# Other landing times, load order and ranks for a list-scheduled attention and feed-forward kernel

## The chip, the cores and the metric

The kernel runs on one core of a Trainium2 chip. It uses five engines: TensorE (PE) for matmuls, VectorE (DVE), ScalarE (ACT) and GpSimd (POOL) for everything elementwise, and SyncE (SP) whose queue issues nearly all DMA transfers. Each engine works through its own list of instructions strictly in order and waits for the others by semaphores. The metric is the device time of one execution in microseconds (us); the median of three runs stands below.

## The reference

The inputs are `q`, `k`, `v` of shape (8, 8, 576, 64), `w_in` (512 x 2048) and `w_out` (2048 x 512), all float32. The output is 4608 x 512 float32.

```python
scores = scale * np.matmul(q, k.transpose(0, 1, 3, 2))
rel = pos[:, None] - pos[None, :]
mask_plain = (rel >= 0) & (rel < 32)                      # heads 0 to 3
mask_dil = (rel >= 0) & (rel < 128) & (rel % 4 == 0)      # heads 4 to 7
attn = softmax(where(masks, scores, -1e9))
x = matmul(attn, v)  # (8, 8, 576, 64) -> (4608, 512)
h = x @ w_in
g = np.maximum(0.01 * h, h)
return g @ w_out
```

## The kernel before

The work is done batch by batch: 8 batches of 8 heads and 576 tokens. A pair of batches gives 1152 columns of the transposed attention output `xt`, which is cut into three chunks of 384 tokens, so there are 12 chunks. For each chunk the up-projection (`up`, matmuls of 128 x 384 at L1073) multiplies `xt` by 16 blocks of `w_in` and ACT bends the result into `gt` (L1084); the down-projection multiplies `gt` by `w_out` and the result is evicted into `osb` or `vst` and stored. The first four tiles of 128 tokens go down in the plain way (`down`, L1244: 16 matmuls of 512 columns in four parts, then an eviction by DVE at L1252). The others go in groups of four through a seven-product scheme (`group`, L1335) that uses sums of blocks of `w_out` (`weight_sums`, L1274). The last four chunks also go up by seven products (`up_seven`, L1157).

Batches 0 and 1 are handled apart ("early"): their q and k are turned by TensorE (L729) and copied into `slots` (L646 on ACT, L648 on DVE), the scores of a unit are made in one bank (L869, L888, L872), exponentiated by ACT (L894), multiplied with v (L929, L949, L939; L917 makes the sums), and normalised through a logarithm and an exponential on ACT (L961, L963) and a product on DVE (L967) that writes `xt`. The 64 tokens beyond 512 of each head come apart: `load_rest` loads those of q and k of all heads in one transfer each, and the last tokens of v of the dilated heads.

All loads arrive as float32 in staging tiles (`stg` for q and k, `vst` for v, parts of `gt`, `wst` and `xt[1]` for the weights) and are cast to float16 by POOL, DVE or ACT (L344, L342). `w_in` comes in eight pieces of 512 KB (`load_w(0..7)`), `w_out` in eight more (`load_w(8..15)`); some pieces share a home buffer with an earlier one and wait until its casts are done. A mask table `late_m` is loaded by SP (`t_near`, L365) and spread by six copies on POOL or ACT (L375).

No order is written out by hand. Every operation is a task with the engines that may do it, an estimated duration, a latency, its dependencies and a priority. `_Plan.run` schedules these tasks as a list scheduler would: for each engine it takes the ready task of lowest priority value, models one DMA server with a service time per transfer (`took`), and gives the landing time of a transfer as its end on the server plus 1.1 us and a lateness. `load` has a factor `slow` on the service time; `load_w` passes `W_SLOW` for the first four pieces of `w_in`. Then `latest` goes backwards through the schedule, ranks every compute task by how late it may start, adds a random disturbance if the seed is not 0, and the plan is run again, once for each entry of `SEEDS`. DMA tasks keep the priorities they were given.

The priorities of the first loads are given by the string `FIRST`, one letter for each step: `b` a group of four heads of batch 0 (q and k), `v` its v, `c` and `y` the same for batch 1, `i` a piece of w_in, `o` a piece of w_out, `0` and `1` the rest tokens of batch 0 and 1. The first `b` and `c` are the dilated heads. `RANKS`, `WHEN`, `MOE`, `W_SUMS` and `SUMS` are first priorities of attention units, of the later batches, of the chunks and of the weight sums; `NEAR` is the priority of the load of `late_m`. Last, where the plan leaves TensorE idle before `WARM` = 62 us of planned time, filler matmuls on a tile of zeros (`warm`, L1558) are put into its list; a few more stand at the beginning (L1454). The resulting lists are what the engines execute.

Of the kernel before, what the change touches and what calls it, by code (L numbers as in the profile page):

```python
# [16 lines left out]
LATE = 7.0  # L17
HOLD = 5.0
W_ENG = ("POOL", "DVE", "ACT")
WHEN = (4.52, -1.03, 5.19, 90.96, 96.86, 93.61, 150.56, 174.24)  # L20
WARM = 62.0
W_SLOW = 1.25
SEEDS = (0, 0, 0, 0, 0, 0, 0, 0, 0, 775539)
AFTER = -1495.0
NEAR = -1498.63
FIRST = 'bvbviiii0iiiicycyoooooooo1'
RANKS = ((12.88, -25.12), (25.21, -10.26), (-1.14, 23.42), (33.7, 4.07))


def _constants():  # L30
# [180 lines left out]
def kernel(  # L211
# [48 lines left out]
    def dram(t, off, *dims):  # L260
        return bass.AP(tensor=t.tensor, offset=t.offset + off, ap=[list(d) for d in dims])
# [67 lines left out]
    def load(queue, dst, src, n, size, deps, prio, slow=1.0):  # L329
        eng = ENG[queue]  # L330
        over = getattr(src if prio == -3000 else dst, "ap", [[0, 0]])[0][1]
        return plan.dma(queue, 0.7 if n == 1152 else 0.62 if over == 64 else 0.45, took(n, size) * slow, deps,
                        lambda e: eng.dma_start(dst, src), prio,  # L333
                        LATE if prio > -1500 + len(FIRST) else 0.8 if prio >= AFTER else 0.0)

# [28 lines left out]
    t_bias = load("ACT", con[:, 128:M_KEEP], const_d[:, 128:M_KEEP], 128, 2 * NBIAS, [], -1498.5)  # L364
    t_near = load("SP", late_m[:, NLATE - 160:NLATE], late_d, 128, 320, [], NEAR)  # L365
    t_con = add("ACT", 0.21, 0.22, [t_bias],
# [161 lines left out]
    def load_rest(b, prio):  # L528


        _, r_old = ring("REST", 1, r_users := [])
        sn, s_old = ring("STG", NST, s_users := [])
        st, lo = stg[sn], []
        for o, src in ((0, q), (1, k)):
            lo.append(load("SP", at(st, 0, 128, o * 256, [1, 256]),
                           dram(src, b * H * HS + 512 * D, [HS, 8], [4 * D, 16], [1, 256]),
                           128, 1024, s_old, prio))
        c = cast(at(rest, 0, 128, 0, [128, 8], [D, 2], [1, D]),
                 at(st, 0, 128, 0, [D, 8], [0, 2], [1, D]), 1024, lo + r_old, prio, W_ENG)
        s_users.append(c)  # L540
        vs, v_old, v_users = v_late[b]
        spread = bass.AP(tensor=vs.tensor, offset=vs.offset + 1024,
                         ap=[[4 * vs.ap[0][0], 16], [256, 4], [1, 256]])
        lv = load("SP", spread,
                  dram(v, (b * H + 4) * HS + 512 * D, [4 * D, 16], [HS, 4], [1, 256]),
                  64, 1024, v_old + [t_vr], prio)
        for vi in (2, 3, 0, 1):
            vt, d_users = kept[b, vi]
            c_v = []
            if vi >= 2:  # L550
                c_v = [cast(at(vt, 0, 64, 0, [1024, 2], [128, 4], [1, D]),
                            at(vs, 0, 64, 1024 + (vi - 2) * 256, [512, 2], [D, 4], [1, D]), 512,
                            [lv] + d_users, prio + 30, W_ENG)]
                v_users += c_v
            visits[b, vi, 1] = rest, [c], r_users, vt, c_v + seen_ones[b, vi], d_users
# [3 lines left out]
    def load_w(n, prio):  # L559
# [6 lines left out]
        if n >= 8:  # L566
            x = 1024 * (n - 8)
            t = load("SP", st, dram(moe_w_out, 128 * x, [2 * DM, 128], [1, 1024]), 128, 4096, old, prio)
            for i in range(2):
# [6 lines left out]
        t = load("SP", st, dram(moe_w_in, n % 4 * 128 * DFF + x, [DFF, 128], [1, 1024]), 128, 4096, old, prio,  # L576
                 W_SLOW if n < 4 else 1.0)
        g, h = n % 4 // 2, n % 2
# [15 lines left out]

    segs = {b: [(0, 96, 384 * (b % 2)), (96, 48, 768 + 192 * (b % 2))] for b in range(EARLY)}
    chunks = [(m, 384 * i, 384) for m in range(B // 2) for i in (0, 1, 2)]
    MOE = 36.21
    PLAIN = 4
    tiles = [(c, tt) for c in range(len(chunks)) for tt in range(3)]
    groups = [tiles[i:i + 4] for i in range(PLAIN, len(tiles), 4)]  # L600
# [1 line left out]
    for m, x, n in chunks:  # L602
        begins.append(begins[-1] + MOE * n / 384)

# [485 lines left out]
        return t_p  # L1090

    SEVEN = (8, 9, 10, 11)
    W_SUMS = 440.23
    u_sums, u_last = {}, {}

    def w_quarter(k, f):
# [2 lines left out]
    def up_sums(old, raw):  # L1099
# [3 lines left out]
        def make(n, dst, x, y, op, deps):  # L1103
            u_sums[n] = shared("DVE", 1.16, 0.2, deps,
                            lambda e: ENG[e].tensor_tensor(out=dst, in0=x, in1=y, op=op),
                            W_SUMS, 0.0, "T")
        w_all = [c for j in range(NJ) for b in w_in_t[j] for c in b]
# [162 lines left out]
    def weight_sums():  # L1270
        w_all = sum((w_out_t[j] for j in range(NJ)), [])

        def minus(n, dst, x, y, deps):
            t_sum[n] = shared("DVE", 1.16, 0.2, deps, lambda e: nc.vector.tensor_tensor(  # L1274
                out=dst, in0=x, in1=y, op=ALU.subtract), SUMS, 0.0, "T")
        minus(1, flat(sums[1]), w_block(0, 1), w_block(0, 0), w_all + w_used[9] + w_used[10])
# [4 lines left out]

    roles = [0, 1]
    last_of = {}
    SUMS = -41.62

    def group(four, acts, at_time, split):

# [175 lines left out]
    ranks = {}  # L1463
    for n, step in enumerate(FIRST):
        seen = FIRST[:n].count(step)
        if step in "io":
# [31 lines left out]
    for m in range(B // 2):  # L1498
        for b in (2 * m, 2 * m + 1):
            if b < EARLY:  # L1500
                attend(b, 0, *RANKS[2 * b])
                if b == 0:
# [3 lines left out]
                    clear_slots(range(4, NT), -700, x_done[0, 0][-1:])  # L1506
                attend(b, 1, *RANKS[2 * b + 1])
            else:
                a, z = WHEN[b - 1], WHEN[b]
                attend(b, None, a, (z - a) / 4)  # L1510
# [40 lines left out]
    order = plan.run()  # L1551
    for seed in SEEDS:
        plan.latest(seed)
# [67 lines left out]
```

## Time and profile before

| | us |
|---|---|
| median of 3 runs | 306.95 (306.02 to 307.24) |
| the profiled execution | 307.09 |
| its span | 305.2 |
| TensorE busy | 293.0 |
| VectorE busy | 249.9 |
| ScalarE busy | 225.1 |
| GpSimd busy | 118.8 |

The span is the time from the first to the last instruction of the profiled execution. Busy times of TensorE include the fillers, and matmuls overlap in their pipeline, so that their ends are modelled; a busy TensorE is no proof of useful work. 47.22 MB are moved by DMA in the execution, 23.39 MB of them in the first 90 us. In the groups of instructions, the up-projections at L1073 hold 97.6 us of TensorE, the seven-product down-projections at L1335 47.2 us with w_out and 16.4 us with the sums in `wst`, and the four plain tiles at L1244 16.1 us. The longest waits in all are POOL's for turned tiles (34.8 us) and ACT's for up-projections (21.3 us); TensorE itself waits little, at most 1.5 us in any one group.

### The profile page before, as it was taken

The page shows a single profiled execution, that of the slowest core. Times are in us where ns is not written, and L with a number is a line of the kernel's source. Part 1 is how long each engine was busy: PE and PEld are TensorE (multiplying, and loading weights), DVE is VectorE, ACT ScalarE, POOL GpSimd, SP SyncE. Part 2 cuts the span into 40 slices and gives each one's busy share as a digit, 9 for nine tenths or more (in the row PEclk, how much of TensorE's full clock was granted, in tenths as well). Part 3 has the DMA queues.
Part 4 walks back from the last instruction along what each step waited for, and adds up shares of the span by engine and source line. Part 5 has one row for each costly group of instructions (what it writes and reads, how often), then busy time and mean ns, then how long its engine had stood idle before and what let it go on. Part 6 is the DMA issues. An engine that isn't in the chain of part 4 may idle for free.

```text
span 305.2 us, 8114 instructions
## 1 busy us (share of the span) xinstructions
PE 293.0 (96%) x3039; PEld 230.5 (76%) x3039; DVE 249.9 (82%) x477; ACT 225.1 (74%) x549; POOL 118.8 (39%) x164
## 2 busy tenths in 40 slices
PE   8788889999999999999999999999999999999994
PEld 4444544566898778778777787778999999999983
DVE  6778785749899989998998899999998868586842
ACT  4989985789898885787677778667568888777420
POOL 6148643058936826936845753771000000000000
PEclk9999999999999999999999999999999999999998
DMA  7999999899799697757994898782212110121034
GB/s 248 336 320 393 312 378 200 171 180 202 173 174 195 134 173 157 138 130 141 177 159 138 148 189 153 143 175 78 73 55 80 42 37 0 37 71 35 11 111 123
DMA packets 157159, 47.22 MB, mean 155 GB/s; under 512 B 137408, under 2 KB 154560, under 8 KB 157120
## 3 DMA queue, kind: packets, MB, share of 16 engines
q1 hardware_dynamic: 156544, 46.39, 64.6%
q8 instruction: 24, 0.39, 0.6%
q10 hardware_dynamic: 576, 0.32, 0.4%
q14 instruction: 15, 0.12, 0.1%
HBM read 37.24 MB, written 9.44 MB: 153 GB/s over the span
## 4 chain that ended last, share of the span: by engine, by line
PE 78%; DVE 6%; ACT 5%; DMA 4%; SPq 3%; issue 1%; DVEq 0%
PE hps L1073 22%; PE fps L1335 21%; PE tp L1335 8%; PE hps L1157 7%; PE fps L1244 5%; PE ops L1016 4%; PE ops L1157 3%; DMA wst<-in_moe_w_in_dram 3%; SPq L333 3%; PE sps L1157 2%; ACT gt L1084 1%; PE sps L1010 1%; PE sps L1016 1%; DVE ee L1026 1%; PE ops L1010 1%
## 5 line engine op out<-in xcount | busy, mean ns | idle before, releaser
L1073 PE MATMUL hps<-xt,w_in 128*128 128x384 f16 (+1 forms) x556 | 97.6, 307 | 1.7 <-DVE w_in L344 1.2
L1335 PEld LDWEIGHTS <-gt 128*128 128x128 f16 x768 | 72.3, 98 | 9.0
L1084 ACT ACTIVATE gt<-hps 128x384 f16<-128x384 f32 (+1 forms) x139 | 62.2, 455 | 22.6 <-PE hps L1073 21.3
L1073 PEld LDWEIGHTS <-w_in 128*128 128x128 f16 x576 | 50.1, 98 | 25.4 <-ACT w_in L342 1.8
L1335 PE MATMUL fps<-w_out,gt 128*128 128x256 f16 x368 | 47.2, 272 | 0.0
L687 POOL COPY slots<-turned 64x512 f16<-64x512 f16 (+1 forms) x36 | 25.7, 715 | 41.2 <-DVE turned L697 34.8
L344 POOL CAST v_all<-vst 64x1152 f16<-64x1152 f32 (+3 forms) x29 | 34.8, 1201 | 7.6 <-DMA vst<-in_v_dram 6.9
L344 POOL CAST nat<-stg 128x576 f16<-128x576 f32 (+1 forms) x44 | 33.8, 789 | 8.0 <-DMA stg<-in_k_dram 3.6
L1026 DVE TENSOR_TENSOR ee<-ee,late_m 128x384 f16<-128x384 f16 (+1 forms) x48 | 29.0, 619 | 3.8 <-ACT ee L1023 3.5
L1045 DVE TENSOR_TENSOR xt<-ops,rc 128x288 f16<-128x288 f32 x48 | 26.5, 553 | 3.7 <-PE ops L1016 2.3
L1157 PEld LDWEIGHTS <-w_in 128*128 128x128 f16 x256 | 21.8, 98 | 0.4
L1364 ACT COPY stg<-fps 128x512 f32<-128x512 f32 (+1 forms) x24 | 12.7, 530 | 11.9 <-PE fps L1335 11.8
L1037 ACT ACTIVATE rc<-rc 128x288 f32<-128x288 f32 x48 | 20.9, 447 | 0.6
L717 DVE STREAM_TRANSPOSE slots<-nat 64x576 f16<-64x576 f16 x24 | 18.4, 767 | 0.4
L697 DVE STREAM_TRANSPOSE turned<-nat 128x576 f16<-128x576 f16 (+1 forms) x24 | 17.5, 735 | 0.4 <-ACT nat L342 0.2
L1157 PEld LDWEIGHTS <-stg 128*128 128x128 f16 x192 | 16.6, 98 | 0.3
L1321 DVE TENSOR_TENSOR gt<-gt 128x1024 f16<-128x1024 f16 x21 | 16.2, 773 | 0.6 <-PE fps L1335 0.6
L1016 PEld LDWEIGHTS <-v_all 128*128 128x128 f16 x240 | 14.5, 98 | 3.0 <-issue 0.2
L1016 PE MATMUL ops<-ee,v_all 128*128 128x96 f16 (+2 forms) x240 | 16.4, 199 | 0.1
L1335 PE MATMUL fps<-wst,gt 128*128 128x256 f16 x128 | 16.4, 273 | 0.0
L967 DVE TENSOR_TENSOR xt<-ops,rc 64x192 f16<-64x192 f32 (+1 forms) x30 | 10.6, 352 | 6.9 <-ACT rc L963 6.4
L1244 PE MATMUL fps<-w_out,gt 128*128 128x512 f16 x64 | 16.1, 380 | 0.0
(151 smaller groups left out, 594.2 us busy)
## 6 DMA issues: line engine op xcount, KB each, us to landing
stg<-in_q_dram SPq DMA_DIRECT2D x48, 144.0 KB, 3.4
stg<-in_k_dram SPq DMA_DIRECT2D x48, 144.0 KB, 3.1
vst<-in_v_dram SPq DMA_DIRECT2D x12, 288.0 KB, 4.1
vst<-in_v_dram SPq DMA_DIRECT2D x24, 128.0 KB, 2.7
gt<-in_moe_w_in_dram SPq DMA_DIRECT2D x5, 512.0 KB, 8.2
xt<-in_moe_w_out_dram SPq DMA_DIRECT2D x3, 512.0 KB, 5.7
gt<-in_moe_w_out_dram SPq DMA_DIRECT2D x3, 512.0 KB, 8.0
vst<-in_v_dram SPq DMA_DIRECT2D x3, 384.0 KB, 6.0
```

The source lines that it names most:

```text
L344: ENG[e].tensor_copy(out=dst, in_=src)
L687: lambda e: (nc.scalar.copy if e == "ACT" else nc.gpsimd.tensor_copy)(out=at(to, p0, p1, p0 if to is qb else 0, *dims), in_=at(fr, p0, p1, ...
L717: lambda e, p0=64 * h: nc.vector.transpose(at(qb, p0, p0 + 64, p0, [128, 9], [1, 64]), na[p0:p0 + 64, S:2 * S]), prio))
L1016: nc.tensor.matmul(at(bk, 0, 128, o, *dims), stationary(s), et[:, c:c + n], start=i == 0, stop=i == len(parts) - 1, skip_group_check=True)
L1026: lambda e: nc.vector.tensor_tensor(out=et[:, 0:w], in0=et[:, 0:w], in1=mk, op=ALU.mult), prio + 0.1)
L1037: lambda e: nc.scalar.activation(out=rt[:, 0:NQ], in_=rt[:, 0:NQ], func=AF.Exp, scale=-1.0),
L1045: lambda e: nc.vector.tensor_tensor(out=dst, in0=at(ot, 0, 128, 0, *src), in1=at(rt, 0, 128, 0, *src), op=ALU.mult), prio + 0.2)
L1073: nc.tensor.matmul(ht[:, 0:n], at(w_in, 0, 128, i * DFF + j // 2 * 256 + j % 2, [2, 128]), at(xt[m % 2], 0, 128, i * 1152 + x0 + x, [1, n] ...
L1084: lambda e: nc.scalar.activation(out=gt[c % NG][:, j * n_c + x:j * n_c + x + n], in_=ht[:, 0:n], func=AF.Prelu, alpha=0.01),
L1157: nc.tensor.matmul(bk[:, 192 * jj:192 * jj + 192], w(i, 2 * jp + jj), x(i), start=first and jj == 0 and i == 0, stop=jj == 1 and i == 1, s ...
L1244: nc.tensor.matmul(ft, g[:, j * n_c + tt * 128:j * n_c + tt * 128 + 128], w_out[:, j * DM:j * DM + DM], start=(j == 0), stop=(j == NJ - 1))
L1335: nc.tensor.matmul(bk[:, x:x + HN], tl[:, off + j * step:off + j * step + 128], rhs(j), start=first and x == 0 and j == 0, stop=j == HJ - ...
```

## The change

The list is told longer times for two kinds of loads: the factor on the first four pieces of `w_in` goes from 1.25 to 1.5, and the loads of the rest tokens of q and k get a factor of 1.8 (1.0 before). The constants that set the first priorities, and the seeds, have other values. In `FIRST`, the loads of batch 1 were `c y c y`, then eight `o`, then the rest tokens; now they alternate with w_out's: `c o o c o y o o o o o y 1`. The priority of the load of `late_m` now puts it ahead of all others on SP's queue. No operation is added or removed, except that the list holds 35 fillers at L1558 instead of 31; what each task computes is the same.

```diff
-WHEN = (4.52, -1.03, 5.19, 90.96, 96.86, 93.61, 150.56, 174.24)
+WHEN = (10.27, -7.79, -8.5, 83.93, 95.4, 101.07, 152.79, 178.8)
 WARM = 62.0
-W_SLOW = 1.25
-SEEDS = (0, 0, 0, 0, 0, 0, 0, 0, 0, 775539)
+W_SLOW = 1.5
+SEEDS = (0, 0, 0, 0, 0, 0, 695242, 808820, 89207, 493360)
 AFTER = -1495.0
-NEAR = -1498.63
-FIRST = 'bvbviiii0iiiicycyoooooooo1'
-RANKS = ((12.88, -25.12), (25.21, -10.26), (-1.14, 23.42), (33.7, 4.07))
+NEAR = -1507.43
+FIRST = "bvbviiii0iiiicoocoyoooooy1"
+RANKS = ((15.99, -23.22), (36.98, -8.41), (1.15, 24.48), (33.14, 4.11))
...
-                           128, 1024, s_old, prio))
+                           128, 1024, s_old, prio, 1.8))
...
-    MOE = 36.21
+    MOE = 39.96
...
-    W_SUMS = 440.23
+    W_SUMS = 379.53
...
-    SUMS = -41.62
+    SUMS = -51.79
```

Since every task goes through the list, the change moves instructions on all engines. On SP: the load of `late_m` is the first of all instead of the fourth; the first two w_out pieces stand after the first q and k of batch 1, the third after the second q and k, then the dilated heads' v, five more w_out pieces, the plain heads' v, and the rest tokens. On TensorE: the first w_out product stands after 18.99 us of matmul work (at 2.4 columns per ns) instead of 24.00, and the parts of the first two tiles alternate; all of chunk 0's plain tiles stand before chunk 1's first up-projection. On ACT: five copies of `late_m` instead of two, before the first cast of k; five casts of q and k of early batches instead of one; two casts of each kind of v instead of one. On DVE: seven casts of q and k instead of ten, two of the rest tokens instead of one, and the first two weight sums around the first tile's eviction.

## The prediction

> **What bounds the kernel now.** I read the busy row by slices first, then a table by stages, then the order of TensorE's work in the start, then the GpSimd casts that show when weights land.
>
> ```profile
> span 305.2 us, 8114 instructions
> ...
> PE   8788889999999999999999999999999999999994
> ...
> DMA  7999999899799697757994898782212110121034
> ```
>
> The span is 305.2 us; this execution took 307.09 us, so 1.9 us lie around it, and it stands 0.14 us above the median of 306.95. TensorE is full from the seventh of the 40 slices (46 us) nearly to the end; the DMA engines are full from the second to the seventh (7.6 to 53 us). The stages (length, then busy time of PE, PE's weight loads, DVE, ACT, POOL, then clock, DMA share, GB/s):
>
> ```profile
> 10.00:20.00 10.00, 7.77 (x84) 4.29 (x80) 6.91 (x20) 9.31 (x30) 2.10 (x3) 1.00 1.08 311
> 20.00:30.00 10.00, 8.63 (x64) 4.61 (x65) 8.55 (x21) 8.22 (x19) 8.19 (x12) 1.00 1.05 379
> 30.00:40.00 10.00, 8.68 (x81) 5.13 (x78) 7.92 (x21) 9.80 (x24) 5.77 (x11) 1.00 1.03 317
> 40.00:50.00 10.00, 9.44 (x86) 5.05 (x85) 7.31 (x20) 7.36 (x24) 3.48 (x6) 1.00 1.03 339
> 50.00:60.00 10.00, 9.96 (x71) 5.28 (x70) 6.40 (x13) 6.03 (x15) 1.22 (x2) 1.00 0.85 158
> 60.00:70.00 10.00, 10.00 (x83) 6.05 (x82) 5.43 (x15) 8.70 (x21) 4.74 (x10) 1.00 0.93 172
> 90.00:120.00 30.00, 29.34 (x339) 23.58 (x338) 28.51 (x47) 24.80 (x62) 16.90 (x20) 1.00 0.89 168
> ```
>
> From 60 us on TensorE only works, with 0.66 us lost in 90 to 120, where VectorE is busy 28.51 of 30. What can move the time is how much work TensorE has behind it when its queue becomes solid. I count that work from the matmuls in instruction order, at 2.4 columns per ns (a row of 8 x 384 columns takes 1.30 us, 2.36 per ns); the whole program has 268.05 us, without the filler products on `warm`, whose time is lost time. The order of TensorE around the first w_out products:
>
> ```profile
> 42.28 0.61 PE L729 MATMUL tp<-con,nat 128*128 128x128 f16 x8 [0.29 <-DVE slots L648]
> ...
> 45.28 0.39 PE L1558 MATMUL fps<-warm 128*128 128x512 f16 x1
> ...
> 46.49 1.04 PE L1244 MATMUL fps<-w_out,gt 128*128 128x512 f16 x4
> ...
> 53.52 0.59 PE L1558 MATMUL fps<-warm 128*128 128x512 f16 x2
> 53.95 1.03 PE L1244 MATMUL fps<-w_out,gt 128*128 128x512 f16 x4
> 54.82 1.46 PE L1073 MATMUL hps<-xt,w_in 128*128 128x384 f16 x8
> ```
>
> Work done: 6.83 us when the first up-projection starts (19.29), 16.64 at 35.4, 24.00 at 46.49, 31.57 at 54.82, 36.6 at 60.0. So 12.5 us are lost before 19.29, 6.3 more up to 35.4, and 4.5 between 35.4 and 54.82 (19.4 of time, 14.9 of work). In that last stretch TensorE has only batch 1's attention, in small steps behind ACT and DVE copies, and the rest of chunk 0's up-projections; w_out comes late:
>
> ```profile
> 38.47 0.61 POOL L344 CAST w_out<-xt 128x512 f16<-128x512 f32 x1 [0.46 <-DMA xt<-in_moe_w_out_dram]
> 39.70 0.61 POOL L344 CAST w_out<-wst 128x512 f16<-128x512 f32 x1 [0.61 <-DMA wst<-in_moe_w_out_dram]
> ...
> 47.53 0.61 POOL L344 CAST w_out<-xt 128x512 f16<-128x512 f32 x1 [0.98 <-DMA xt<-in_moe_w_out_dram]
> 50.13 0.61 POOL L344 CAST w_out<-xt 128x512 f16<-128x512 f32 x1 [1.99 <-DMA xt<-in_moe_w_out_dram]
> 51.55 0.61 POOL L344 CAST v_all<-vst 64x512 f16<-64x512 f32 x1 [0.80 <-DMA vst<-in_v_dram]
> ```
>
> Each cast waits for its own landing: one 512 KB piece per 1.2 to 1.3 us, the last of eight at 50.1, batch 1's last v tokens at 51.5.
>
> **The start of batch 0 (cost).** The mask load late_m goes from fourth to first on SP's queue. SP's issues are 0.51 us apart (0.75, 1.26, 1.77), so the first two q loads and the first k load come 0.5 us later; those behind keep their places. ACT now builds five of the six pieces of late_m, and builds them ahead of its cast of the first k. POOL took 1.01 us for the four pieces that it had; ACT took 0.97 for its two. With three more (384 columns to the 672 of those two, so 0.55) all five take some 1.5 us from 4.1, so the k cast starts near 5.6, not 4.86. Everything of batch 0's first scores queues behind it. ACT also takes two more casts of q and k before 20 us (0.62 each) against one 0.63 copy that goes to DVE; with 9.31 of 10 us busy it has no room. So the first up-projection comes 0.7 us late, near 20.0. What hides it: the third and fourth pieces of w_in, whose casts waited for landings until 20.66 and 22.17, unchanged by the edit. But the list puts four fillers (0.86 us) there instead of one (0.21), and they run whether or not the weights are in. Bounds: 0 (landings decide) to 1.1 (nothing hides it). I take 0.6, nearer the unhidden end, since the copies of the rest tokens and the second w_in casts are chained behind the same products.
>
> **q, k of batch 1 and the w_out pieces (gain).** The DMA engines are full, so landings only permute. At 1.3 us a piece from 27.75, when w_in's last piece landed: batch 1's first q and k near 30.4 as now, then w_out 1 and 2 near 33, the second q and k at 35.6 (1.2 later than now), w_out 3, the dilated heads' v at 38.2 (now 31.9), w_out 4 to 8 until 44.7 (now 50.1), the plain heads' v at 47 (now 37.0). The casts of today's second and third piece lie 2.4 us apart (39.70, 42.08), so such a stumble may add 1 to 3 us to the last ones. The first w_out product stands at 18.99 us of work instead of 24.00, and all of chunk 0's three plain tiles (48 x 512 columns, 10.2 us) before any of chunk 1's. From 35.4 + 0.6 = 36.0 TensorE then has this to go through until the first up-projection of chunk 1, which stands at 36.6 us of work: 36.6 - 16.6 = 20.0 us of work. To it come three losses. Five score units, which set the pace until w_out is there, took 8.76 us (35.81 to 44.57) and now have 7.6 us of work between them: 1.1. The third tile needs the first one's bank, copied by DVE (0.68) behind a weight sum (1.21), while TensorE has 1.0 of other work: 0.3. And chunk 1 needs the last plain heads' normalised rows, which now stand right ahead of it: from values at 52.36 the log, exponential and product ended at 53.87, 1.5 us, of which the list fills 1.06 with fillers. Sum: 36.0 + 20.0 + 1.1 + 0.3 + 1.5 = 58.9, against 60.0: 1.1 us gained.
>
> **Queues.** POOL: its cast of the fourth head pair's q and k now stands behind the clearing of slots, which waits for TensorE's scores (2.11 us, until 32.27 today); the next casts behind it are w_out's, wanted only near 36, so this costs nothing unless the scores slip by more than 3 us. ACT: the cast of the last plain v stands ahead of four log/exp pairs; TensorE reaches these only near 53.4 and the landing is 47 to 50: nothing, unless it lands after 52. SP: the first output stores stand earlier, between batch 2's loads, at about 56; the tiles they store are evicted by 52 to 57: nothing.
>
> **The middle and the end.** Batch 2's scores stand at 51.2 us of work instead of 49.3, and DVE has one weight sum (1.2) and one eviction (0.7) less ahead of it. The order of batches 2 to 7 is shuffled locally by other seeds; the last 14 products are the same. The gain is bounded by the 0.66 us lost in 90 to 120; a loss by the longest run of DVE work that TensorE could be put behind, two masks and a sum, 2.0 us. I take 0.
>
> **Sum.** 305.2 - 1.1 = 304.1 of span, 306.0 with the 1.9 around it, 305.9 from the median.
>
> [...]
>
> **Rivals.** (1) Faster: the start's delay is wholly hidden behind w_in's landings (0.6) and the middle gives back its 0.66: 305.9 - 1.3 = 304.6. For it: TensorE already waits for these casts at 20.01 and 28.31. Against: ACT's 9.31 and 9.80 of 10. (2) Slower: DVE's list puts the first weight sum, which waits for w_out's last piece, ahead of the first tile's eviction, and TensorE's third tile waits for that bank. TensorE wants it near 51.5; less eviction, sum and cast (0.68, 1.21, 0.61) the piece must have landed by 49.0, and each us later costs one. At today's 50.1 plus one stumble of 2.4 it lands at 52.5: 3.5 us, 309.4. For it: the DMA engines are full and the queue carries the same bytes by then. Against: 768 KB of v now follow w_out instead of leading it (2.6 us today, from the landing of the last k at 34.4 to that of the last v at 37.0), and today's last piece was issued only at 44.33, when its buffer was freed by a DVE cast at 43.85, which POOL now does early. (3) No change: ACT becomes the bound. It gets 1.6 us more of casts and copies up to 60 us; if all of it is felt the start costs 1.6, not 0.6. From 36.6 to 43.5 us of work, now with fewer w_out products between, ACT has 8 activations at 0.37 (starts at 23.97, 24.35, 24.72), 4 exponentials at 0.38, 4 logs at 0.51, 2 inverses at 0.41 and a cast of 0.56, 7.9 us, for TensorE's 6.9: 1.0 more. 307.9. Against: in 60 to 70 ACT is busy 8.70 and TensorE waits for nothing.
>
> **Numbers.** Forecast 0.37, rival 1 0.25, rival 2 0.18, rival 3 0.20. A measurement of this kernel tells about 0.5% (1.5 us) from no change. Rival 1 (304.6) is faster, the forecast and rival 3 lie within but for their edges, rival 2 is slower; faster: 0.25 + 0.07 of the forecast; slower: 0.18 + 0.06 of rival 3; same: 0.44. The range reaches from 1.2 beyond rival 1 to just past rival 2's price; the forecast's own is 304.9 to 306.9.
>
> **What would show it.** Right: first up-projection near 20.0; first L1244 near 38; L1244 solid to 56; a wait or fillers of 1 to 1.6 us before chunk 1's first L1073 near 58.9; from there the same time to the end, 242 us. Wrong: a first up-projection at 19.3 (step one), L1244 waiting for w_out or a bank by more than 0.5, a v cast after 52, or more than 1 us lost after 60.

## The result, and the profile after

| | kernel before | changed kernel |
|---|---|---|
| median | 306.95 us (7 runs, 305.37 to 307.24) | 308.43 us (7 runs, 307.58 to 309.37) |
| ratio, with its interval | | 1.0068 [1.0042, 1.0094] |
| profiled execution | 307.09 | 308.43 |
| its span | 305.2 | 306.4 |

The changed kernel is slower by 0.68%, 2.1 us. Its busy rows by slices:

```profile
span 306.4 us, 8119 instructions
...
PE   7779899899999999999999999999999999999995
...
DMA  6999997989989888766993998782222110022034
```

TensorE (PE) is emptier in the first three slices than before (777 for 878). The table by stages (length, then busy time of PE, its weight loads, DVE, ACT, POOL, then clock, DMA share, GB/s) says where:

```profile
10.00:20.00 10.00, 7.72 (x88) 4.52 (x89) 6.58 (x19) 9.26 (x28) 1.22 (x2) 1.00 1.03 299
20.00:30.00 10.00, 8.52 (x55) 4.39 (x54) 9.24 (x23) 6.53 (x17) 5.86 (x9) 1.00 1.05 374
30.00:40.00 10.00, 8.13 (x77) 4.78 (x75) 7.42 (x19) 9.80 (x22) 7.47 (x14) 1.00 1.06 404
40.00:50.00 10.00, 10.00 (x90) 5.96 (x88) 7.26 (x21) 8.46 (x24) 3.77 (x6) 1.00 0.88 287
50.00:60.00 10.00, 9.77 (x78) 5.07 (x76) 7.42 (x14) 5.32 (x16) 0.92 (x2) 1.00 0.94 176
60.00:70.00 10.00, 9.06 (x76) 5.41 (x74) 6.32 (x18) 8.86 (x23) 2.19 (x7) 1.00 0.85 173
```

From 40 to 50 TensorE is now solid (9.44 before), but 60 to 70, which was solid, has lost 0.94 us. What these rows don't show is how much of the work is done by then. The next table is worked out from the traces as in the prediction: the matmuls in order of their start, without the fillers of L1454 and L1558, at 2.4 columns per ns (in both traces most of L1073's matmuls, 384 columns each, begin 0.16 us apart); each column is the time at which so much work had been begun. head20 and head20_norm are experiments told below.

```
work    before   after   after-before   head20   head20_norm
 1        7.27    7.88      +0.6          7.59       7.27
 7       19.35   20.83      +1.5         19.63      19.38
10       23.79   26.16      +2.4         24.25      24.01
16.6     35.30   38.32      +3.0         36.41      36.18
24       46.32   46.76      +0.4         44.88      44.61
36       59.36   58.73      -0.6         56.85      56.58
36.6     59.98   61.72      +1.7         59.82      58.40
100     127.17  129.47      +2.3        127.46     125.79
260     292.33  294.62      +2.3        292.61     290.94
```

The start loses 3.0 us until 16.6 us of work. The stretch behind it wins 3.6 and is ahead of the kernel before at 36. Then 0.6 us of work takes 2.99 us (0.62 before): this is the wait for batch 1's norms ahead of chunk 1. From there the loss stays between 1.6 and 2.8 us, and from 90 us of work on between 2.1 and 2.5. (The spans differ by only 1.2, because what follows 260 us of work took 1.1 us longer in the profiled run of the kernel before; the last section tells of it.)

The start, in POOL's first casts of w_in:

```profile
17.45 0.61 POOL L344 CAST w_in<-gt 64x512 f16<-64x512 f32 x1 [11.26 <-DMA gt<-in_moe_w_in_dram]
...
21.38 0.79 POOL L344 CAST w_in<-wst 64x512 f16<-64x512 f32 x1 [2.02 <-DMA wst<-in_moe_w_in_dram]
23.10 0.61 POOL L344 CAST w_in<-wst 64x512 f16<-64x512 f32 x1 [0.94 <-DMA wst<-in_moe_w_in_dram]
```

All wait for the transfer itself. They stood at 15.16, 20.68 and 22.20 before: the landings came 0.7 to 2.3 us later, though SP issues the same loads in the same order but for the mask. Single traces scatter here: casts and norm (told below), whose lists up to there are those of the changed kernel, have the third piece at 20.85 and 20.22 and the first up-projection at 20.19 and 20.54, where the changed kernel has 21.38 and 20.77. Over all traces shown in this document, nine with late_m first and nine with it fourth, this cast stood at 20.8 and 20.4 in the mean, that of the fourth piece at 22.9 and 22.0.

The chain of work that ended last, followed back from the end of the program, says what the start waited for. Before, it runs along SP's queue into the landing of w_in's fourth piece:

```profile
12.49 9.65 DMA wst<-in_moe_w_in_dram
```

In the changed kernel it runs from the first v load (issued at 3.23 us, ahead of all others of v), which landed at 9.50 (7.95 before), through the lists of ACT and DVE, and through no landing of w_in:

```profile
3.23 6.27 DMA vst<-in_v_dram
9.52 0.63 ACT v_all L342
...
21.70 0.74 DVE w_in L344
23.59 0.42 DVE w_in L344
```

The w_out pieces, on the other hand, came early, in the forecast order (first cast 38.47 before, last 50.13):

```profile
36.18 1.30 POOL L344 CAST w_out<-xt 128x512 f16<-128x512 f32 x2
...
46.39 0.62 POOL L344 CAST w_out<-xt 128x512 f16<-128x512 f32 x1 [0.63 <-DMA xt<-in_moe_w_out_dram]
```

TensorE ahead of chunk 1, whose first up-projection is the last line:

```profile
58.81 0.25 PE L917 MATMUL ops<-ee,ones 128*64 128x192 f16 x2
59.30 0.33 PE L872 MATMUL sps<-slots 128*128 128x96 f16 x4 [0.23 <-DVE slots L648]
59.46 0.81 PE L1558 MATMUL fps<-warm 128*128 128x512 f16 x3
61.12 0.59 PE L1558 MATMUL fps<-warm 128*128 128x512 f16 x2 [0.84 <-DVE osb L1252]
61.59 0.33 PE L872 MATMUL sps<-slots 128*128 128x96 f16 x4
61.76 1.56 PE L1073 MATMUL hps<-xt,w_in 128*128 128x384 f16 x7
```

and ACT in the same time, with DVE's copies of one kind below it:

```profile
59.28 0.26 ACT L646 COPY slots<-tp 64x128 f16<-64x128 f16 x1 [0.28 <-DVE slots L648]
59.82 0.26 ACT L646 COPY slots<-tp 64x128 f16<-64x128 f16 x1 [0.28 <-DVE slots L648]
60.10 0.55 ACT L961 ACTIVATE rc<-ops 128x192 f32<-128x192 f32 x2
60.54 0.62 ACT L963 ACTIVATE rc<-rc 128x192 f32<-128x192 f32 x2
```

```profile
59.02 0.22 DVE L648 COPY slots<-tp 64x128 f16<-64x128 f16 x1 [0.33 <-ACT slots L646]
59.57 0.22 DVE L648 COPY slots<-tp 64x128 f16<-64x128 f16 x1 [0.33 <-ACT slots L646]
```

The values of the last plain heads are there at 59.06 (58.81 and 0.25). Their logarithms stand on ACT behind slot copies which ACT and DVE make in turns, each waiting for the other's: 0.54 us for a copy of 0.26. The logarithms start at 60.10, and TensorE has only fillers in the meantime. By the plan's own start times these eight copies run side by side on the two engines in 0.9 us, and the five fillers stand behind them.

### The profile page after: what moved, and what is told of

Its sections match the earlier page's. It is cut to its first block, busy times and chain, and to the rows that moved or that the text cites. A ratio compares the mean times of both kernels' runs of the same rounds, so it can differ in the third digit from the quotient of the medians.

```text
span 306.4 us, 8119 instructions
## 1 busy us (share of the span) xinstructions
PE 293.2 (96%) x3043; PEld 230.6 (75%) x3043; DVE 248.6 (81%) x482; ACT 224.3 (73%) x548; POOL 117.1 (38%) x160
## 3 DMA queue, kind: packets, MB, share of 16 engines
q1 hardware_dynamic: 156544, 46.39, 63.8%
HBM read 37.24 MB, written 9.44 MB: 152 GB/s over the span
## 4 chain that ended last, share of the span: by engine, by line
PE 81%; DVE 8%; ACT 6%; DMA 2%; issue 1%; SPq 1%; DVEq 0%
PE hps L1073 23%; PE fps L1335 21%; PE tp L1335 8%; PE hps L1157 7%; PE fps L1244 4%; PE ops L1016 4%; PE ops L1157 3%; DMA vst<-in_v_dram 2%; PE sps L1157 2%; ACT slots L646 1%; PE sps L1016 1%; DVE gt L1321 1%; PE sps L1010 1%; PE ops L1010 1%; PE ops L1335 1%
## 5 line engine op out<-in xcount | busy, mean ns | idle before, releaser
L1073 PE MATMUL hps<-xt,w_in 128*128 128x384 f16 (+1 forms) x556 | 97.6, 307 | 0.5 <-ACT gt L1084 0.2
L1073 PEld LDWEIGHTS <-w_in 128*128 128x128 f16 x576 | 49.7, 97 | 24.4 <-issue 2.1
L687 POOL COPY slots<-turned 64x512 f16<-64x512 f16 (+1 forms) x36 | 27.4, 762 | 43.5 <-DVE turned L697 42.4
L344 POOL CAST v_all<-vst 64x1152 f16<-64x1152 f32 (+1 forms) x26 | 32.7, 1256 | 11.2 <-DMA vst<-in_v_dram 6.5
L1026 DVE TENSOR_TENSOR ee<-ee,late_m 128x384 f16<-128x384 f16 (+1 forms) x48 | 23.6, 499 | 2.9 <-ACT ee L1023 2.5
L1037 ACT ACTIVATE rc<-rc 128x288 f32<-128x288 f32 x48 | 21.6, 449 | 0.6
L1364 ACT COPY stg<-fps 128x512 f32<-128x512 f32 (+1 forms) x22 | 11.6, 526 | 8.2 <-PE fps L1335 8.0
L1016 PEld LDWEIGHTS <-sides 128*128 128x128 f16 x240 | 14.3, 98 | 3.5 <-issue 0.7
L1321 DVE TENSOR_TENSOR gt<-gt 128x1024 f16<-128x1024 f16 x21 | 16.9, 807 | 0.0
L1167 ACT COPY rc<-hps 128x384 f32<-128x384 f32 x23 | 11.0, 478 | 7.1 <-PE hps L1157 5.8
```

Source lines behind the costliest of these rows:

```text
L344: ENG[e].tensor_copy(out=dst, in_=src)
L687: lambda e: (nc.scalar.copy if e == "ACT" else nc.gpsimd.tensor_copy)(out=at(to, p0, p1, p0 if to is qb else 0, *dims), in_=at(fr, p0, p1, ...
L1016: nc.tensor.matmul(at(bk, 0, 128, o, *dims), stationary(s), et[:, c:c + n], start=i == 0, stop=i == len(parts) - 1, skip_group_check=True)
L1026: lambda e: nc.vector.tensor_tensor(out=et[:, 0:w], in0=et[:, 0:w], in1=mk, op=ALU.mult), prio + 0.1)
L1037: lambda e: nc.scalar.activation(out=rt[:, 0:NQ], in_=rt[:, 0:NQ], func=AF.Exp, scale=-1.0),
L1073: nc.tensor.matmul(ht[:, 0:n], at(w_in, 0, 128, i * DFF + j // 2 * 256 + j % 2, [2, 128]), at(xt[m % 2], 0, 128, i * 1152 + x0 + x, [1, n] ...
```

## The experiments

The kernel before was timed again with each group of experiments, at medians of 306.19 to 306.39 us; the ratios below go by these. "1 us of work" and the like are read as in the table above.

The first theory was that the loss is made in the first 6 us, by late_m. Four kernels, which edit the finished order and leave the rest of the list as it was. `sp` is the list of SP's tasks in order, `late_mask` the six copies that make late_m.

**near_fourth.** The changed kernel with the load in its old place and the copies behind the first k:

```diff
+    t_near.start = sp[3].start + 1e-4
+    copy = [t for t in act if t.start > late_mask[4].start and t not in late_mask][1]
+    for i, t in enumerate(late_mask):
+        t.start = max(t.start, copy.start + 1e-4 * (i + 1))
```

> The changed kernel with the one load of late_m put back to the fourth place of SP's queue and its copies on ACT put back behind the first cast of k and its first slot copy; everything else stays in the changed order. Theory A (the loss is made in the first 6 us: 40 KB at the head of the queue and five copies ahead of the first cast of k): first up-projection near 19.5 instead of 20.77, 16.6 us of TensorE's real work done near 36.5 instead of 38.2, and 306.0 to 306.9 us, at or below the kernel before. Theory B (the loss is in the new list order and load order between 8 and 36 us, whatever the first load is): first up-projection earlier by some tenths at most, 16.6 us of work still near 38, and 308.0 to 308.8 us.

Measured: 309.56 us, 1.0109 [1.0083, 1.0135] of the kernel before: neither theory. The five copies now stood between the casts of the first and of the second k on ACT; 1 us of work was done at 8.13 (7.88 in the changed kernel). So it put the load back and delayed the second k instead (its cast stood at 7.87, 7.26 in the changed kernel).

**masks_behind.** The same without the first line of the diff.

> The changed kernel with late_m's load still first on SP, but its copies on ACT behind the first cast of k and its first slot copy. If within theory A the copies on ACT are what counts, the first up-projection comes near 20.0 and the time falls to 307.0 to 307.5; if the transfer at the head of the queue counts, it stays at 308.0 to 308.5 with the first up-projection near 20.5. Theory B: 308.0 to 308.8 as well.

Measured: 309.88, 1.0114 [1.0082, 1.0145]; the first up-projection at 22.16, 1 us of work at 8.54. Also worse; in its profiled run TensorE's clock stood at 0.50 from 9.07 to 12.48 us besides (last section); two of its six runs have a mean clock of 0.994, the four others 1.000.

**near_first.** The kernel before, its late_m load first:

```diff
+    t_near.start = sp[0].start - 1e-4
```

> The kernel before with late_m's load alone put first on SP, its copies where they were. Theory A with the transfer as the cause: SP's three v loads end near 11.0 instead of 9.7, first up-projection near 20.3 instead of 19.29, time 307.8 to 308.4. Theory B: 0 to 0.4 us over the kernel before, 306.9 to 307.4.

Measured: 306.83, 1.0017 [1.0000, 1.0034]: 0.5 us, if anything. Landings came about 1 us later, as theory A had it (the last of the three v loads that SP issues one after another from 6.3 us on, called the third v load below, at 14.27; 13.37 before), but the first up-projection stood at 19.46, and the time hardly moved.

**near_first_masks.** The same, and five copies on ACT where the changed kernel has them:

```diff
+    t_near.start = sp[0].start - 1e-4
+    for i, t in enumerate(late_mask[:5]):
+        t.eng, t.start = "ACT", t_con.start + (1e-4 * i if i else -1e-4)
```

> The kernel before with late_m's load first on SP and the five copies on ACT in the places that the changed kernel gives them. Theory A: first up-projection near 20.7, 308.0 to 308.8, all of the loss. Theory B: at most 0.6 us over the kernel before (the 0.74 us by which the first cast of k comes later, partly covered), 307.0 to 307.6.

Measured: 307.56, 1.0040 [1.0020, 1.0060]. The first up-projection stood at 21.14, 1.9 us late, of which TensorE had won back 0.5 by 16.6 us of work. So late_m with its copies is a part of the loss, 1.2 of 2.1 us, and not all. The next four kernels looked for the place in the list.

**head8, head20.** The changed kernel, with the tasks that the kernel before plans before 8 or 20 us on that kernel's engines and in its order. `to` holds engine and start of these 79 or 182 tasks by their number, which is the same in both kernels.

```diff
+    for i, t in enumerate(order):
+        if t.n in to:
+            t.eng, t.start = to[t.n]
+            t.dur = dict(t.choices)[t.eng]
+        else:
+            t.start = max(t.start, 20 + 1e-4 * i)
```

> The changed kernel whose first 79 tasks of the plan (the first 8 planned us on all five engines: late_m's load and copies, the first casts, turns and slot copies) stand on the engines and in the order of the kernel before; everything behind them in the changed order. Theory A2 (the start is lost in these tasks, and a change that moves only late_m does not undo it, because the casts of q and k changed engines too): first up-projection near 19.6 instead of 20.77, 16.6 us of real TensorE work done near 36.8 instead of 38.3, 306.8 to 307.3 us. Theory B (the start is lost in the order behind 8 us): first up-projection 20.3 or later, 16.6 us of work near 38, 308.0 to 308.8 us.

Measured: 308.54, 1.0074 [1.0050, 1.0099]: nothing won. Its profiled run had the first up-projection at 19.61 and stood 0.8 us ahead of the changed kernel's at 100 us of work, but over six runs that is not in the time.

> The same with the first 182 tasks (20 planned us, up to the first up-projections). Theories A2 and B both put the first up-projection near 19.4. If what the start loses is carried to the end, 16.6 us of work is done by 36.0 to 36.6, chunk 1's first up-projection comes near 59.7 and the time is 306.0 to 306.6. Theory C (TensorE between 38 and 59 us stands so close to the landings and to the chain of batch 1 that an earlier start is used up by waits): chunk 1's first up-projection at 61 or later, 307.6 to 308.6 us.

Measured: 306.97, 1.0020 [1.0001, 1.0039]: 1.5 us of the loss are gone. Chunk 1's first up-projection at 59.86. So a loss of the start is carried to the end (theory C falls), and undoing it needs the list between 8 and 20 us as well. At 16.6 us of work head20 is still 1.1 us behind the kernel before: of the 3.0 there, 1.9 belong to the first 20 planned us and the rest to the order behind them, which does other work first and has won it back by 24.

**first20_after.** The reverse: the kernel before with the changed order of the first 20 planned us.

> The kernel before whose first 20 planned us stand on the engines and in the order of the changed kernel. If the start's loss is carried on: first up-projection near 20.8, and 1.5 to 2.1 us over the kernel before, 308.3 to 309.0. Theory C: some of it is used up by waits that were there anyway, 307.0 to 307.8.

Measured: 308.61, 1.0080 [1.0059, 1.0101]. The first 20 planned us alone make the kernel before as slow as the whole change does.

**norm.** Meant to bring the norms forward, as norm2 below, but with the two multiplications (380, 386) moved up instead of the eviction (492) down:

```diff
+    for n in (380, 386):
+        of[n].start = of[492].start - 0.002 + 1e-4 * n / 386
```

> The changed kernel with one place edited, the norms ahead of chunk 1: the four slot copies that ACT makes in turns with DVE ahead of the logarithms go to DVE, the two norm multiplications stand ahead of the eviction, and the five fillers there are left out. Theory N (the wait before chunk 1 is longer than the 1.2 us that the plan filled, since copies that the plan lets run side by side on two engines wait for one another): chunk 1's first up-projection at 60.8 to 61.1 instead of 61.76, and 0.6 to 1.0 us off the changed kernel, 307.4 to 307.9. Rival: what follows is late anyway and the wait moves to it, 308.2 to 308.7.

Measured: 310.32. In this kernel the two multiplications stood ahead of the logarithms, so that they take the reciprocals of other units; the time doesn't answer the question.

**norm2.** The changed kernel with four slot copies (395 to 417) from ACT to DVE, DVE's eviction and memset (492, 744) behind the second norm multiplication (386), and without the five fillers:

```diff
+    for n in (395, 396, 415, 417):
+        of[n].eng = "DVE"
+    for i, n in enumerate((492, 744)):
+        of[n].start = of[386].start + 0.001 * (i + 1)
+    order = [t for t in order if t.kind != "w" or not 56 < t.start < 58]
```

> The changed kernel with the norms ahead of chunk 1 brought forward: the four slot copies that ACT makes in turns with DVE go to DVE, the eviction and one memset on DVE stand behind the two norm multiplications, the five fillers there are left out. In the changed kernel the last value matmul ends at 59.06, ACT's logarithms start at 60.10 behind the copies and chunk 1's first up-projection at 61.76. Theory N: that wait of 2.4 us is part of the loss; the logarithms start near 59.3, the up-projection 0.7 to 1.0 us earlier against the work done before it, and 0.6 to 1.0 us come off the changed kernel's 1.0068 of the kernel before: 1.0035 to 1.005. Rival: another wait takes its place, 1.006 to 1.008.

Measured: 307.96, 1.0036 [1.0017, 1.0055]. Theory N holds: the work from 36 to 36.6 us took 1.83 us instead of 2.99. The edit changes three things at once; which of them it needs is not separated. (The start of its profiled run is not to be compared: the clock stood at 0.50 there from 8.91 to 12.32 us.)

**casts.** The changed kernel with one cast of w_in's fourth piece (61) from DVE to ACT and DVE's six memsets behind its last cast of that piece (59):

```diff
+    of[61].eng, of[61].start = "ACT", of[62].start + 0.001
+    for i, t in enumerate(sets):
+        t.start = of[59].start + 0.001 * (i + 1)
```

> The changed kernel with one place edited, the casts of the second half of w_in's first 1024 columns: one cast of the last staged piece goes from DVE to ACT, which is idle there until 26.06, and DVE's six memsets of slots stand behind its three casts. Theory D (between the first and the second half of the first up-projections TensorE waits for DVE, which the list gives four of these casts and the memsets): the up-projections behind the fillers start at 24.4 to 24.8 instead of 25.38, 0.5 to 0.8 us come off: 1.004 to 1.0055 of the kernel before. Rival: the next landing of w_in or of batch 0's rest holds TensorE as long, 1.006 to 1.008.

Measured: 308.24, 1.0062 [1.0037, 1.0087]. In its trace the work from 9 to 10 us took 1.88 us instead of 2.25 (1.70 before); in the time, with this interval, 0.4 us can't be told from nothing. Theory D explains a small part at most.

**told.** The kernel before with the longer landing times alone, planned anew:

```diff
-W_SLOW = 1.25
+W_SLOW = 1.5
...
-                           128, 1024, s_old, prio))
+                           128, 1024, s_old, prio, 1.8))
```

> The kernel before with the longer landing times alone (1.5 for w_in's first four pieces, 1.8 for the last tokens of q and k); load order, ranks and seeds as before, and the plan made anew. The plan's own end goes from 298.19 to 301.59, and to 300.66 with all of the change: by the plan the other parts win back 0.93. Theory P (the list follows what it is told: it puts the work behind the landings later, and TensorE runs in list order whether a piece is there or not): first up-projection 0.5 to 1.0 later than in the kernel before, 1.005 to 1.010. Rival: told times change little in the list that the chip notices, 0.999 to 1.003.

Measured: 311.07, 1.0136 [1.0110, 1.0161], more than either expected. The first up-projection comes 1.1 us later than before, though late_m is loaded fourth and the first landings are those of the kernel before (third v load 13.22); of that 0.7 us fall between 14.56 and 17.98, where the clock stood at 0.50. But 60 us of work are only 2.0 us late and 80 are 4.9 late. That the ranks and seeds, which were drawn for another plan, no longer fit there is my reading; no run tests it. As a price for told times alone it is too high.

**first_new.** The kernel before with the new `FIRST` alone, planned anew:

```diff
-FIRST = 'bvbviiii0iiiicycyoooooooo1'
+FIRST = "bvbviiii0iiiicoocoyoooooy1"
```

> The kernel before with the new load order alone (w_out's pieces among batch 1's loads), the plan made anew with the old times, ranks and seeds. By the plan 38 us of TensorE work stand at 54.14 instead of 56.04, but chunk 1's start stays where it was (56.68 and 56.69) and the end moves from 298.19 to 300.59. Theory W (what the new order gains ahead of chunk 1 is lost again in a wait for batch 1's norms): 36 us of work done 1 to 2 us earlier than in the kernel before, 36.6 us of work at the same time or later, 1.003 to 1.009 with the plan's later stages. Rival (my forecast's gain of the alternation is there once the start is as before): 0.995 to 0.998.

Measured: 313.34, 1.0212 [1.0183, 1.0241]; most of that is again behind chunk 1's start. Ahead of it the case is clean: 16.6 us of work at 34.42 (35.30 before), 36 at 58.10 (59.36), then 36.6 at 61.11 (59.98). TensorE ahead of chunk 1:

```profile
58.18 0.25 PE L917 MATMUL ops<-ee,ones 128*64 128x192 f16 x2
...
58.83 0.81 PE L1558 MATMUL fps<-warm 128*128 128x512 f16 x3
60.55 0.59 PE L1558 MATMUL fps<-warm 128*128 128x512 f16 x2 [0.92 <-DVE osb L1252]
...
61.15 1.60 PE L1073 MATMUL hps<-xt,w_in 128*128 128x384 f16 x7
```

It is the same picture as in the changed kernel, with the old start. So the wait belongs to the load order: theory W.

The last four asked whether the two places add up.

**head20_norm.** The edits of head20 and norm2 together.

> head20 and norm2 in one kernel: the changed kernel with the kernel before's first 20 planned us and with the norms ahead of chunk 1 brought forward. If the two places are separate and are the whole loss: 1.002 less 0.003, that is 0.998 to 1.000 of the kernel before, chunk 1's first up-projection near 58.8 (before 60.0). Rival: an earlier start and an earlier norm use up the same slack, 1.001 to 1.003.

Measured: 304.96 us, 0.9955 [0.9941, 0.9970]: faster than the kernel before by 1.4 us, and the fastest of all. TensorE and, below it, ACT ahead of chunk 1:

```profile
56.87 0.33 PE L872 MATMUL sps<-slots 128*128 128x96 f16 x4
58.27 0.33 PE L872 MATMUL sps<-slots 128*128 128x96 f16 x4 [1.07 <-ACT ee L894]
58.44 1.46 PE L1073 MATMUL hps<-xt,w_in 128*128 128x384 f16 x8
```

```profile
56.78 0.55 ACT L961 ACTIVATE rc<-ops 128x192 f32<-128x192 f32 x2 [1.68 <-PE ops L917]
57.22 0.62 ACT L963 ACTIVATE rc<-rc 128x192 f32<-128x192 f32 x2
```

The logarithms now start when the values are there, and chunk 1 at 58.44; 36.6 us of work are begun 1.6 us earlier than in the kernel before. Together the two edits bring 3.5 us off the changed kernel, more than their 1.5 and 1.0 alone, but the intervals are too wide to say that they help each other.

**mixed.** head20_norm with the edit of casts.

> The same with the edit of casts as well (one cast of w_in's fourth piece on ACT instead of DVE, DVE's memsets behind its casts). TensorE's 100 us of work were done 1.2 us earlier in norm2 and 0.4 us earlier in casts than their starts allow in the changed kernel, so from head20's 127.5 that is 125.9, against 127.2 in the kernel before: 0.995 to 0.998. Rival: the landings hold TensorE at the next piece, 0.998 to 1.001.

Measured: 305.46, 0.9976 [0.9953, 0.9999]; no better than head20_norm, so the casts show no gain here either.

**mixed_first.** mixed with late_m's load (3) first on SP, ahead of the first q (107):

```diff
+    of[3].start = of[107].start - 1e-4
```

> mixed with late_m's load put first on SP, and nothing else moved. All loads behind it should land 1.0 to 1.3 us later, as in the runs that had it first. If TensorE's work up to chunk 1 is bound by landings, that goes to the end: 0.003 to 0.004 above mixed. If the list's order binds, it costs what it cost the kernel before in near_first, 0.001 to 0.002.

Measured: 306.02, 0.9998 [0.9982, 1.0013], 0.0022 above mixed with intervals that overlap, near what near_first cost. The landings were late by more: the third v load at 14.94 instead of 13.25.

**list8_20.** The kernel before with the changed order of the tasks between 8 and 20 planned us alone, written as in head20.

> The kernel before with the changed order only in the tasks between 8 and 20 planned us (casts of w_in, slot copies, scores and norms of batch 0's first units); its first 8 us and everything behind 20 as it was. If these tasks hold half of first20_after's 1.008: 1.003 to 1.005. If they cost only together with late landings: 0.999 to 1.002. If they hold all of it: 1.006 to 1.009.

Measured: 307.48, 1.0041 [1.0024, 1.0058]: half of first20_after's 1.0080; near_first_masks (1.0040) is the other half.

## Why the forecast was wrong

I forecast 305.9, a gain of 1.1 at chunk 1's first up-projection; there was a loss of 1.8 there and of 2.3 from 100 us of work on.

**The start of batch 0 (cost): the step that failed.** I took 0.6 us at 16.6 us of work, within bounds of 0 and 1.1. The trace has 3.0. Two sentences of it were wrong. "The first two q loads and the first k load come 0.5 us later; those behind keep their places": the order of their issues did, but the landings came later, the first v load by 1.55 us (9.50 for 7.95) and the third by 1.56 (14.93 for 13.37). And "what hides it: the third and fourth pieces of w_in ... unchanged by the edit": these casts, too, came later, from 20.68 and 22.20 to 21.38 and 23.10 (0.4 and 0.9 us in the means over nine traces each), so the cover went along with what it was to cover. It moved less than the rest, and no longer decided: the chain of the changed kernel runs through the v load and the lists of ACT and DVE, and 7 us of work were begun 1.5 us late. The late copies on ACT were rightly seen (the first k was cast at 5.92, forecast 5.6), but their price with the load is 1.2 us in the end (near_first_masks), and the list between 8 and 20 us, for which I had only 0.86 us of fillers, costs as much again (list8_20). Put back, the first 20 us bring 1.5 us of time and 1.9 of the 3.0 (head20). Which of the tasks between 8 and 20 us it is, is not settled: casts took the most likely ones and found little. Nor why head8 won nothing.

**"The DMA engines are full, so landings only permute".** True for the w_out pieces: the second landed at 34.7 and the last at 46.3, forecast 33 and 44.7, about as late as the third v load ahead of them; and the stretch they feed was well estimated: the first w_out product stood at 41.54 (forecast near 38), and from there TensorE had no gap over 0.3 us until 59. From 16.6 us of work to 36 I had 20.8 us (36.0 to 56.8 by the forecast's terms), the trace has 20.4, and the kernel before needed 24.1. Not true at the very start: from 2 to 3 us the engines were busy 0.45 to 0.65 (rows of mixed and mixed_first below), not yet full.

**The norms ahead of chunk 1: right place, too small.** I took 1.5 us beside the work; it was 2.4 (2.99 for 0.6 us of work). I took the row of an undisturbed chain, log to product, of one unit, where two stand together (0.55, 0.62 and 0.62 us for log, exponential and product, against 0.33, 0.36 and 0.36 in my row), and did not look at what ACT and DVE had to do ahead of it: eight slot copies, which the plan lets run side by side and which wait for one another in the trace. norm2 shows that 1.2 us of this wait can be taken away, with the copies, the eviction and the fillers changed together.

**The middle and the end.** I took 0; from chunk 1 to 100 us of work another 0.6 us was lost (1.7 to 2.3 in the table). Where, no run asked.

**Sum.** Forecast -1.1; start +2.4 more than taken, middle stretch -0.4, norms +0.9, behind chunk 1 +0.6: +2.4, against 2.3 in the table; the rest is rounding. With the old start and the norms brought forward, the gain that the load order was given is there: head20_norm begins 36.6 us of work at 58.40 instead of 59.98, 1.6 us ahead, and is 1.4 us faster.

**The rivals.** Rival 2 gave a slower time, but its mechanism did not come: w_out's last piece was cast at 46.39, before the 49.0 from which it would have decided, and no product of the third tile waited for a bank. Rival 3, ACT as the bound, is not it either: ACT was busy 5.32 of 10 us in 50 to 60, and what it cost there was the order of its list, not its load. Rival 1's hidden start was the opposite of what happened. The clock was 1.00 in every stage of the changed kernel up to 242 us, at least 0.998 over each of its seven runs, and its longest gap between matmuls 0.89 us; the clock plays no part in its loss. In the profiled runs of four experiments it fell to 0.50 for a time, with 1.93 us of idle TensorE at most, in all, in the 3.41 us before, as the last section tells.

## What to carry to other kernels

A stall may be called hidden behind a transfer only if the edit does not move the transfer too; trace the cover back to its issue. A load order that pulls work forward wins only as far as the next thing that waits for the loads pushed back: here the norms of batch 1, which gave back 2.4 of 3.6 us. Constants and seeds found by search seem to belong to one plan: the told times or the load order changed alone, without a new search, cost 1.4 and 2.1% here, most of it in stages that these do not concern. No run made the search anew, so that a search would win it back is not shown.

## What the runs showed of the hardware

**A small transfer at the head of the queue.** late_m is 128 rows of 320 bytes, 40 KB. In nine traces with it first, the third v load landed at 14.27 to 15.58 us (mean 14.80); in nine with it fourth, at 13.12 to 13.93 (mean 13.46): 1.3 us, for a load that by an estimate from its size and the 379 GB/s that the next us shows should take about 0.1 us. The rows of mixed for 2 to 4 us, columns as above:

```profile
2.00:3.00 1.00, 1.00 (x4) 0.30 (x2) 0.69 (x5) 0.03 (x1) 1.00 (x3) 1.00 0.45 138
3.00:4.00 1.00, 1.00 (x4) 0.34 (x3) 0.80 (x4) 0.00 (x0) 1.00 (x3) 1.00 1.10 379
```

and of mixed_first, which differs in nothing else:

```profile
2.00:3.00 1.00, 1.00 (x4) 0.30 (x2) 0.69 (x5) 0.03 (x1) 1.00 (x3) 1.00 0.65 79
3.00:4.00 1.00, 1.00 (x4) 0.34 (x3) 0.81 (x4) 0.00 (x0) 1.00 (x3) 1.00 0.99 332
```

The engines are busier from 2 to 3 us and move fewer bytes, 79 GB/s for 138. In this pair the lag is made early: the second k load lands at 7.71 for 6.35, the first v load at 9.49 for 7.83, the third at 14.94 for 13.25, so from the first v load on it stays at 1.7 us. Why it is so large these runs don't say.

**The stores at the end.** From 260 us of work to the end of the span took 11.7 to 11.9 us in most profiled runs and 12.7 to 13.1 in five, with the same instructions. SP's last six stores, first in the kernel before, then in the changed one:

```profile
297.94 4.82 SPq L333 DMA_DIRECT2D out_dram<-vst  x6
```

```profile
300.25 3.72 SPq L333 DMA_DIRECT2D out_dram<-vst  x6
```

The issue of the same six takes 1.1 us longer in the one. A comparison of two single profiled runs by their span is wrong by so much; by the work done at a given time it is not. Each kernel has one profiled run here, so whether this goes with the execution or with the kernel is open.

**Four runs in which the clock fell to 0.50.** In the profiled runs of masks_behind, norm2, told and norm the granted clock fell to 0.50 in the middle of the work, for 3.41 us in the first three and for 6.83 us in norm. (In the kernel before and in the changed one it stands at 1.00 from its first record on and falls to 0.50 only behind the last matmul, at 303.40 and 305.31 us.) masks_behind, the 3.41 us before the fall and those at 0.50:

```profile
5.66:9.07 3.41, 1.48 (x16) 0.86 (x14) 1.51 (x4) 2.99 (x9) 0.32 (x1) 1.00 1.05 356
9.07:12.48 3.41, 3.41 (x24) 1.80 (x24) 1.86 (x5) 2.54 (x7) 0.00 (x0) 0.50 1.15 312
```

What the four have in common is that TensorE was busy for 1.48, 1.70 (norm2), 1.76 (norm) and 1.82 us (told) of the 3.41 before the fall, 43 to 53%, so that its idle time there was 1.93 us at most in all; norm2's longest wait in it is 1.34 us, for ACT, until 8.94. Stretches of that length behind which the clock stayed at 1.00 were busier: 1.95 us at 11.25 in the kernel before and 1.93 at 12.80 in the changed one (57%), the least busy of each from 5 to 79 us, and in first_new

```profile
42.80:46.20 3.40, 1.88 (x26) 1.14 (x26) 1.97 (x6) 2.48 (x7) 1.38 (x3) 1.00 0.94 229
46.20:49.60 3.40, 3.40 (x28) 1.66 (x27) 2.50 (x8) 3.02 (x10) 0.36 (x1) 1.00 0.72 167
```

with 55%. In norm TensorE was busy for 2.40 us, 70%, of the first 3.41 at 0.50, and the clock stayed at 0.50 for another 3.42. What sets the fall and the return these runs don't show.

In masks_behind the two runs with a mean clock of 0.994 took 310.45 and 311.45 us, the four others 309.52 in the mean: 1.4 us. Over all experiments 17 runs had a mean clock of 0.992 to 0.995; they took 1.0 us more in the mean than the runs of the same kernel at 0.997 and above.

In the first microseconds the column of the clock shows 1.00 without a record; the records begin at 4.9 us in the changed kernel and at 6.4 in the kernel before. The fillers at the start (L1454, 512 columns each) begin 0.43 us apart, 1.2 columns per ns, in both; two of L1558, as long, begin 0.22 us apart at 5.98 us in the changed kernel.

**Two engines that copy in turns.** Slot copies of 64 x 128 that ACT and DVE share came every 0.54 us from each engine, while one of them takes 0.26 on ACT and 0.22 on DVE. Each waits for a semaphore that the other engine's copy raises, so this is the order that the program sets; whether the engines could copy side by side without it no run shows. In the kernel before, three of them in a row on DVE took 0.67 us (58.40). With all eight on DVE (norm2) the logarithms started at 60.45, 0.1 us after the last matmul of the values had begun.
